# Fused attention and gated feed-forward, one core: second x rows on ScalarE's queue, the rest of the opening in order on SyncE's, short warm-up products up to the transposes, last rows divided at column 384

## Chip, cores, metric

One Trainium2 (trn2) chip, one core. The metric is the device time of the program in microseconds (us). Each chip job also timed the kernel before on its own chip, so comparisons below are made inside one job.

## The reference, cut to what matters

```python
xn = layernorm(x)                       # x: 2048 rows of 640
s  = attention(xn, k_cache, v_cache, wq, wo)   # 32 heads of 192, window 512
g  = silu(B(xn))                        # B: (sigmoid(xn @ w_gate) * (xn @ w_up)) @ w_down
return x + s * g
```

Inputs and output are bfloat16. The kernel starts with the layernorm and the B branch for the first 512 rows, and ends with the projection by `wo`, the product with the gate, and the addition of what is accumulated.

## The kernel before: the parts that the change touches

The opening loads, and the order in which the engines are given work (cut; `...` marks cuts):

```python
def load_x(t, n):
    x = xpool.tile([P, n, D], BF16, ...)
    nc.sync.dma_start(x[:], xf[t * P:(t + n) * P, :]...)
...
nc.vector.memset(warm[:], 0.0)
nc.vector.memset(wg_sb[:, 0, 0:2], 0.0)      # 0.95 to 1.01 us; ScalarE's DMA is issued at 1.06
load_x(0, 1)                                 # SyncE
load_x(1, 1)                                 # SyncE
load_f(nc.scalar, wg_sb, wg_r, 0, 4, 0, 3)   # ScalarE, 384 KB
load_f(nc.sync, wg_sb, wg_r, 0, 4, 3, NCD)
load_f(nc.sync, wu_sb, wu_r, 0, 4, 0, 3)
load_x(2, 1)
load_f(nc.sync, wu_sb, wu_r, 0, 4, 3, NCD)
load_x(3, 1)
...
dummy(18)               # warm-up: 18 products of 256 columns; nothing reads them
stats_half(0, 0); stats_half(0, 1)
stats_end(0)            # aggregate, sqrt on ScalarE, stats_half(1, 0), then the reciprocal
normal(0, ...)          # xn of rows 0
stats_half(1, 1)
turn_pe(0)              # five transposes on TensorE, copies to xnT
dummy(2)
...
m0 = tile_gates(0, 3)   # 20 products with w_gate, 20 with w_up
```

The last four row tiles (`last_rows`) are projected in two halves of 320 columns each. VectorE multiplies each half with the gate (`gated_rows`), and adds the accumulated rows one step later (`stored_rows`), after which the half is written.

The softmax here doesn't subtract the row's maximum and nothing guards it: scores larger than these inputs give would overflow.

## Time and profile before

| | before |
|---|---|
| timed | 924.52 us median of 3 (924.49 to 924.56) |
| the profiled execution | 922.88 us, span 921.08 us |
| PE busy | 913.9 us of 921.1 |
| rows 0 usable / rows 1 used | 3.06 / 4.99 us |
| transposes start / first gate product | 6.01 / 6.92 us |
| last product ends / VectorE ends | 917.14 / 918.48 us |

From the page of the kernel before, the span and the busy time (share of the span, number of instructions):

```profile
span 921.1 us, 25176 instructions
PE 913.9 (99%) x11438; PEld 630.7 (68%) x11456; DVE 490.7 (53%) x983; ACT 302.7 (33%) x333; POOL 132.7 (14%) x157
```

TensorE (PE) is busy nearly throughout; only the two ends can give anything. The timeline of VectorE at the opening of the kernel before (start, duration, engine, line, operation, output<-inputs; in brackets the idle time before it and what ended it):

```profile
3.06 0.89 DVE L198 BATCH_NORM_STATS2 st<-x_sb 128x6 f32<-128x320 bf16 x2 [2.04 <-DMA x_sb<-in_A_x_dram]
3.98 0.21 DVE L203 BATCH_NORM_AGGREGATE mv<-st 128x2 f32<-128x12 f32 x1
4.99 0.49 DVE L198 BATCH_NORM_STATS2 st<-x_sb 128x6 f32<-128x320 bf16 x1 [0.79 <-DMA x_sb<-in_A_x_dram]
5.40 0.15 DVE L208 RECIPROCAL rstd<-rstd 128x1 f32<-128x1 f32 x1
5.58 0.64 DVE L218 TENSOR_SCALAR xn<-x_sb,mv,rstd 128x384 bf16<-128x384 bf16 x2
```

The statistics of rows 1 wait 0.79 us for their DMA, and they stand ahead of the reciprocal that rows 0 need. TensorE over the same time:

```profile
1.06 4.02 PE L190 MATMUL bank<-warm 128*128 128x256 bf16 x18 [1.06 <-DVE eps_t L182]
6.01 0.54 PE L230 MATMUL bank<-ident,xn 128*128 128x128 bf16 x5 [0.93 <-DVE xn L218]
6.92 1.28 PE L300 MATMUL bank<-xnT,wg_sb 128*128 128x128 bf16 x20
8.04 0.83 PE L300 MATMUL bank<-xnT,wu_sb 128*128 128x128 bf16 x12
```

Two things are to be read here. There is a hole of 0.93 us between the warm-up products and the transposes. And the products run at two paces. The 18 warm-up products of 256 columns start 213 ns apart. The 20 gate products of 128 columns take from 6.92 to 8.04, 56 ns apart. The first pace is about half of the second: 256 columns at 56/128 ns each would take about 112 ns. The trace's clock record (kept in the packed trace; no view prints it) has the change between the two: it rises to 1.0 at 5.60 us after the start of the span, and falls to 0.5, 914.772 us after that. "Half clock" below means the slower pace. The changed kernel's trace has the same 914.772 us between rise and fall; three later traces, with a rise at 10 us or after, have 911.359 us there, 3.413 us less. What sets the moment of the rise the traces don't show.

The end of VectorE's work in the kernel before:

```profile
917.20 0.48 DVE L473 TENSOR_TENSOR o_sb<-bank,gate 128x320 f32<-128x320 f32 x1
917.60 0.88 DVE L478 TENSOR_TENSOR gate<-o_sb,acc 128x320 bf16<-128x320 f32 x2
```

After the last product (ended at 917.14) come one product with the gate and two additions of 320 columns.

### The profile page before, as it was taken

To read this page: it belongs to the slowest core of one execution; us is meant where nothing else is said; L and a number is where in the kernel's file an instruction comes from. 1 tells how busy PE (TensorE), PEld (TensorE's weight loads), DVE (VectorE), ACT (ScalarE), POOL (GpSimd) and SP (SyncE) were. 2 spreads that over 40 slices of the span, in tenths; PEclk is the share of its full clock that TensorE was granted. 3 is DMA by queue.
4 is the path that set the end of the run, shared out by engine and by line. 5 is a ranking of instruction groups with operands and counts; after the bars stand their busy time and mean duration, and the time that the engine had idled before them with its cause. 6 is when DMAs were issued, how large, how long until landed. Compare 5 with 4: busy or idle time off the path is not lost.

```text
span 921.1 us, 25176 instructions
## 1 busy us (share of the span) xinstructions
PE 913.9 (99%) x11438; PEld 630.7 (68%) x11456; DVE 490.7 (53%) x983; ACT 302.7 (33%) x333; POOL 132.7 (14%) x157
## 2 busy tenths in 40 slices
PE   8999999999999999999999999999999999999998
PEld 6445455466868686767677777777776767686885
DVE  5452522445646464655555555555464646464667
ACT  4222222254242424233333333242414151515150
POOL 1000100001002000200120011001100111065733
PEclk9999999999999999999999999999999999999999
DMA  9310330115344524352425162526252614263435
GB/s 318 83 28 2 89 86 1 43 62 87 71 70 103 89 55 85 92 100 42 98 79 113 36 104 79 113 30 111 64 106 49 114 61 93 63 116 107 91 80 135
DMA packets 163147, 77.14 MB, mean 84 GB/s; under 512 B 140992, under 2 KB 158608, under 8 KB 163040
## 3 DMA queue, kind: packets, MB, share of 16 engines
q1 hardware_dynamic: 155680, 53.64, 29.8%
q0 software_dynamic: 5808, 20.52, 7.9%
q8 instruction: 89, 1.46, 0.7%
q10 hardware_dynamic: 1552, 1.38, 0.5%
q14 instruction: 18, 0.15, 0.1%
HBM read 39.45 MB, written 2.62 MB: 46 GB/s over the span
## 4 chain that ended last, share of the span: by engine, by line
PE 98%; DVE 1%; DMA 0%; issue 0%; ACT 0%; DVEq 0%; SPq 0%
PE bank L492 22%; PE bank L421 21%; PE bank L443 19%; PE bank L403 18%; PE bank L250 10%; PE bank L262 6%; PE bank L369 1%; PE bank L300 1%; PE bank L526 0%; DMA x_sb<-in_A_x_dram 0%; DVE gate L478 0%; DVE o_sb L473 0%; DVE st L198 0%; PE bank L230 0%; DVE xn L218 0%
## 5 line engine op out<-in xcount | busy, mean ns | idle before, releaser
L407 ACT ACTIVATE E<-bank 128x1024 bf16<-128x1024 f32 x256 | 255.6, 1023 | 456.2 <-PE bank L403 456.1
L421 PE MATMUL bank<-xnT,wq_sb 64*128 64x512 bf16 x1800 | 226.5, 376 | 0.0
L492 PE MATMUL bank<-wo_sb,oT 64*128 64x320 bf16 x2688 | 205.3, 296 | 0.0
L403 PE MATMUL bank<-qT,kT 64*128 64x512 bf16 x1536 | 200.9, 376 | 0.0
L443 PE MATMUL bank<-vbuf,E 64*128 64x193 bf16 x4096 | 195.4, 243 | 0.0
L443 PEld LDWEIGHTS <-E 64*128 64x128 bf16 x4096 | 179.0, 94 | 9.9 <-issue 0.3
L492 PEld LDWEIGHTS <-oT 64*128 64x128 bf16 (+1 forms) x2892 | 164.3, 94 | 29.8 <-issue 0.3
L428 DVE CAST qT<-bank 128x1024 bf16<-128x1024 f32 x90 | 110.2, 1225 | 128.5 <-PE bank L421 128.5
L421 PEld LDWEIGHTS <-wq_sb 64*128 64x128 bf16 x1800 | 106.6, 100 | 86.5 <-issue 0.4
L403 PEld LDWEIGHTS <-kT 64*128 64x128 bf16 x1536 | 88.7, 94 | 72.9
L456 DVE TENSOR_TENSOR o_st<-bank,rden 128x768 bf16<-128x768 f32 x128 | 122.6, 958 | 4.8 <-DMA out_dram<-gate 0.4
L507 DVE TENSOR_TENSOR acc<-bank,acc 128x640 f32<-128x640 f32 x96 | 79.1, 824 | 20.1 <-PE bank L492 20.1
L118 POOL DMA_DIRECT2D vbuf<-in_A_v_cache_dram x28 | 21.1, 755 | 311.0 <-PE bank L443 308.1
L426 DVE COPY seen<-bank 128x2 f32<-128x2 f32 x90 | 14.3, 159 | 79.1 <-PE bank L421 79.1
L455 DVE RECIPROCAL rden<-bank 128x4 f32<-128x4 f32 x128 | 23.4, 183 | 60.4 <-PE bank L443 59.5
L250 PE MATMUL bank<-xnT,wu_sb 128*128 128x512 bf16 x215 | 54.4, 379 | 0.3
L250 PE MATMUL bank<-xnT,wg_sb 128*128 128x512 bf16 x216 | 54.5, 379 | 0.2
L256 DVE TENSOR_TENSOR hT<-bank,sig 128x512 bf16<-128x512 f32 x44 | 30.3, 689 | 42.9 <-ACT sig L253 42.9
L262 PE MATMUL bank<-wd_sb,hT 128*128 128x128 bf16 (+1 forms) x376 | 52.4, 297 | 0.4
L253 ACT ACTIVATE sig<-bank 128x512 bf16<-128x512 f32 x44 | 26.3, 598 | 68.3 <-PE bank L250 66.8
L262 PEld LDWEIGHTS <-hT 128*128 128x128 bf16 x384 | 29.7, 98 | 23.1
L250 PEld LDWEIGHTS <-wu_sb 128*128 128x128 bf16 x220 | 21.5, 98 | 26.0
(56 smaller groups left out, 364.2 us busy)
## 6 DMA issues: line engine op xcount, KB each, us to landing
wo_sb<-in_A_wo_dram SPq DMA_DIRECT2D x7, 960.0 KB, 5.7
wq_sb<-in_A_wq_dram POOLq DMA_DIRECT2D x7, 960.0 KB, 6.2
k_st<-in_A_k_cache_dram POOLq DMA_DIRECT2D x14, 384.0 KB, 5.6
vbuf<-in_A_v_cache_dram POOLq DMA_DIRECT2D x28, 192.0 KB, 3.4
row<-in_A_x_dram POOLq DMA_DIRECT2D x16, 160.0 KB, 3.0
oT<-o_st SPq DMA_TRANSPOSE x128, 3.4
x_sb<-in_A_x_dram SPq DMA_DIRECT2D x3, 640.0 KB, 10.6
wd_sb<-in_B_w_down_dram SPq DMA_DIRECT2D x1, 1920.0 KB, 14.2
```

Source lines behind the costliest of these rows:

```text
L250: nc.tensor.matmul(bank[k][:, half, 0:r1 - r0], lhsT=w[:, c, f * P:(f + 1) * P], rhs=xnT[:, b, c, r0:r1], start=(c == 0), stop=(c == NCD - 1))
L253: nc.scalar.activation(sig[:, 0:r1 - r0], bank[k][:, 0, 0:r1 - r0], AF.Sigmoid)
L256: nc.vector.tensor_tensor(hT[b][:, f, r0:r1], bank[k][:, 1, 0:r1 - r0], sig[:, 0:r1 - r0], ALU.mult)
L262: nc.tensor.matmul(wide(k)[:, d0:d1], lhsT=hT[b][:, f, q * P:(q + 1) * P], rhs=wd_sb[:, f, d0:d1], start=(f == 0), stop=(f == NF - 1))
L403: nc.tensor.matmul(bank[k][:, i, :], lhsT=kT[r, pr, j, c * P:(c + 1) * P], rhs=q[r, pr * DJ + j, :], start=(j == 0), stop=(j == DJ - 1))
L407: nc.scalar.activation(E[u, pr][:, c, :, :], bank[k][:], AF.Exp, scale=scale_qk)
L421: nc.tensor.matmul(bank[k][:, half, :], lhsT=wq[r, c, col:col + DJ * (P - 1) + 1:DJ], rhs=xnT[r, b, c, :], start=(c == 0 and not second), ...
L428: nc.vector.tensor_copy(qT[u][:, 2 * m:2 * m + 2, :], bank[k][:])
L443: nc.tensor.matmul(o4[:, q, 0:DH + 1], lhsT=e[r, c, h % 2, q * P:(q + 1) * P], rhs=vbuf[r, h, c, 0:DH + 1], start=(turn == 0 and qq == 0 a ...
L456: nc.vector.tensor_tensor(o_st[u][:, :, h * DH:(h + 1) * DH], o4[:, :, 0:DH], rden[:].to_broadcast([P, TQ, DH]), ALU.mult)
L492: nc.tensor.matmul(res[:, half, :], lhsT=oT[u][r, cc, q * P:(q + 1) * P], rhs=wo[r, cc, half * HD:(half + 1) * HD], start=(turn == 0 and c ...
L507: nc.vector.tensor_tensor(cols(acc[:, t, :]), res, cols(acc[:, t, :]), ALU.add)
```

## The change

The intent is to have rows 1 earlier, to leave no hole between warm-up and transposes, and to shorten what follows the last product. Rows 1 move to ScalarE's queue and the first gate weights to SyncE's; six short products follow the 18 long ones; the last row tile is cut 384 + 256 instead of 320 + 320, and one more addition goes to GpSimd.

```diff
-        def load_x(t, n):
+        def load_x(t, n, eng=nc.sync):
...
-            nc.sync.dma_start(x[:], xf[t * P:(t + n) * P, :].rearrange("(q p) d -> p q d", p=P))
+            if eng is nc.scalar:
+                nc.vector.memset(x[:, 0, 0:2], 0.0)
+            eng.dma_start(x[:], xf[t * P:(t + n) * P, :].rearrange("(q p) d -> p q d", p=P))
...
-        nc.vector.memset(wg_sb[:, 0, 0:2], 0.0)
         load_x(0, 1)
-        load_x(1, 1)
-        load_f(nc.scalar, wg_sb, wg_r, 0, 4, 0, 3)
+        load_x(1, 1, nc.scalar)
+        load_f(nc.sync, wg_sb, wg_r, 0, 4, 0, 3)
...
         dummy(18)
+        dummy(6, 64)
...
+            cut = HD if q < TQ - 1 else 384
-            for i in range(2):
-                d0, d1 = i * HD, (i + 1) * HD
+            for i, (d0, d1) in enumerate(((0, cut), (cut, D))):
...
-                args = (o, t, d0, d1, nc.vector if q or i else nc.gpsimd, (nc.scalar, nc.sync)[i])
+                wait.append((o, t, d0, d1, nc.gpsimd if n in (0, 4) else nc.vector, (nc.scalar, nc.sync)[i]))
-                while len(wait) > (1 if (q, i) > (0, 0) and (q, i) < (TQ - 1, 1) else 0):
+                while len(wait) > (n in (1, 2, 3, 6)):
```

More of the change, by code (lines that the diff above doesn't have):

```diff
@@ L186, with dummy @@
         nc.gpsimd.memset(vbuf[:, :, :, DH:DH + 2], 1.0)
-        def dummy(n):
+        def dummy(n, cols=256):
             for _ in range(n):
-                nc.tensor.matmul(bank[1][:, 1, 0:256], lhsT=warm[:, 0:P], rhs=warm[:, 0:256],
+                nc.tensor.matmul(bank[1][:, 1, 0:cols], lhsT=warm[:, 0:P], rhs=warm[:, 0:cols],
                                  start=True, stop=True)
@@ L521, in last_rows @@
             o = fin.tile([P, D], F32, name="o_sb", bufs=2)
-            for i in range(2):
-                d0, d1 = i * HD, (i + 1) * HD
-                k = order[(2 * q + i) % 4]
+            cut = HD if q < TQ - 1 else 384
+            for i, (d0, d1) in enumerate(((0, cut), (cut, D))):
+                n = 2 * q + i
+                res = bank[order[n % 4]][:, 0, 0:d1 - d0]
                 for cc in range(GC):
-                    nc.tensor.matmul(bank[k][:, 0, 0:HD],
-                                     lhsT=oT[NU - 1][:, cc, q * P:(q + 1) * P],
+                    nc.tensor.matmul(res, lhsT=oT[NU - 1][:, cc, q * P:(q + 1) * P],
                                      rhs=grp[NG - 1]["wo"][:, cc, d0:d1],
                                      start=(cc == 0), stop=(cc == GC - 1))
-                gated_rows(o, t, d0, d1, bank[k][:, 0, 0:HD])
-                args = (o, t, d0, d1, nc.vector if q or i else nc.gpsimd, (nc.scalar, nc.sync)[i])
-                wait.append(args)
-                while len(wait) > (1 if (q, i) > (0, 0) and (q, i) < (TQ - 1, 1) else 0):
+                gated_rows(o, t, d0, d1, res)
+                wait.append((o, t, d0, d1, nc.gpsimd if n in (0, 4) else nc.vector,
+                             (nc.scalar, nc.sync)[i]))
+                while len(wait) > (n in (1, 2, 3, 6)):
                     stored_rows(*wait.pop(0))
```

## The prediction

> **What bounds it now.** The profile's first part has TensorE (PE) busy 913.9 of 921.1 us; the chain of waits is 98% PE. The timeline shows no PE gap over 0.06 us between 10 us and the end, so only the two ends can give anything, and what PE gains at the opening should reach the end undiminished.
>
> Opening (timeline, chain, waits): x rows 0 are usable at 3.06. The first half statistics of rows 1 wait for their DMA until 4.99 (0.79 us of idle; issue at 1.15, landing 3.8 us later) and stand, in VectorE's order, ahead of the reciprocal (5.40) that rows 0 need. ScalarE's square root was done at 4.53. Then xn 5.58, transposes 6.01 (PE idle 0.93 us after the warm-up products), copy 6.53 to 6.87, first gate product 6.92. The chain shows just this sequence. The packets show why rows 1 are late: ScalarE's queue carries the 384 KB of gate weights issued at 1.06, which share the 16 DMA engines with rows 1 until 4.5; both finish together.
>
> **What changes.** Rows 1 (160 KB) go on ScalarE's queue, the gate weights on SyncE's behind rows 0. [...] At the pace of the ScalarE queue now, 128 packets were through by about 3.5, so I estimate rows 1 landing at 3.9 to 4.3 instead of 4.96. Gate weights still land near 5.3, needed at 6.2.
>
> VectorE then runs statistics of rows 1 right after its aggregate (4.20), reciprocal at about 4.61, i.e. 0.79 earlier; ScalarE's root allows at most 0.84. Transposes could start near 5.22. The warm-up products end at 4.87 (start to start 213 ns, half clock until 5.60 in the profile); six more of 64 columns fill to about 5.2 to 5.5 (estimate, 53 to 107 ns each). If the clock still rises at 5.60, some transposes run at half clock and end at about 5.8 instead of 6.35. So the copy starts near 5.87 and the first gate product near 6.25: 0.65 us earlier. Up-weights (landing 7.12, 8.32) are needed from 7.4 and 8.3, rows 2 and 3 (7.58, 8.77) at 7.6 and 8.8: just in time, a loss of at most 0.1 there, partly absorbed by the 0.13 us wait at 9.73. The DMA stream is full (350 GB/s), so this is where a larger gain would end.
>
> Tail (timeline): last product ends 917.14; then product with the gate (0.40 start to start at 320 columns), two additions (0.40 + 0.48), end 918.48; write landed 920.10; span 921.08. With 384/256 columns these become about 0.34 + 0.47 + 0.42: 0.07 less; moving one addition to GpSimd unloads VectorE where it wasn't late.
>
> **Prediction.** 0.65 + 0.07, about 0.7 us: 923.8 us; range 923.3 to 924.2. Faster by over 2%: 0.005; within 2%: 0.99; slower: 0.005.
>
> **What would show it.** Rows 1's statistics start at 4.2 with no DMA wait; reciprocal 4.6; PE gap before the transposes under 0.3; first gate product 6.2 to 6.3; last product about 0.65 earlier; VectorE's end 1.27 after it (now 1.34).
>
> **What would make it wrong.** Rows 1 land no earlier [...]; the short products run past xn; the clock rises at another time in the timed runs, where continuous products could gain more; up-weights arrive later and PE waits; or the ends vary by some tenths.

## The result

The changed kernel took 922.65 us (median of 4, 922.58 to 922.98), the kernel before 924.54 us (median of 4, 924.49 to 924.91; three of them are those quoted above). The ratio is 0.9979, 95% interval 0.9962 to 0.9997. (A ratio is the mean time of one kernel's fast runs over that of the other's of the same rounds, so not quite the ratio of the medians quoted.) The gain is 1.89 us, where 0.72 had been predicted and 924.2 to 923.3 was the range. Yet the two profiled executions differ by only 0.30 us in the time of the run (922.88 against 922.58), and by 0.27 in the span. The page of the changed kernel:

```profile
span 920.8 us, 25187 instructions
PE 914.8 (99%) x11444; PEld 629.1 (68%) x11462; DVE 491.2 (53%) x982; ACT 302.3 (33%) x333; POOL 133.5 (15%) x158
```

So two questions had to be answered: why the timed runs gained 1.9 us, and why the profiled ones gained 0.3 rather than 0.7. VectorE's timeline of the changed kernel:

```profile
4.05 0.21 DVE L204 BATCH_NORM_AGGREGATE mv<-st 128x2 f32<-128x12 f32 x1
4.17 0.44 DVE L199 BATCH_NORM_STATS2 st<-x_sb 128x6 f32<-128x320 bf16 x1
4.62 0.16 DVE L209 RECIPROCAL rstd<-rstd 128x1 f32<-128x1 f32 x1
```

Rows 1 are there (all 16 parts of the DMA had landed at 3.49, before 4.96) when the aggregate is done; the wait is gone and the reciprocal starts 0.78 us earlier. TensorE's timeline of the changed kernel:

```profile
1.06 4.34 PE L191 MATMUL bank<-warm 128*128 128x256 bf16 x24 [1.06 <-DVE eps_t L183]
5.25 0.71 PE L231 MATMUL bank<-ident,xn 128*128 128x128 bf16 x5
6.20 1.28 PE L301 MATMUL bank<-xnT,wg_sb 128*128 128x128 bf16 x20
7.62 0.84 PE L301 MATMUL bank<-xnT,wu_sb 128*128 128x128 bf16 x12
```

There is no hole before the transposes, and the first gate product starts at 6.20 instead of 6.92. But the up-weight products start at 7.62, only 0.42 earlier than before. The weight loads in the timeline of the changed kernel name the reason:

```profile
7.62 0.67 PEld L301 LDWEIGHTS <-wu_sb 128*128 128x128 bf16 x12 [0.32 <-DMA wu_sb<-in_B_w_up_dram]
8.82 0.45 PEld L301 LDWEIGHTS <-wu_sb 128*128 128x128 bf16 x8 [0.25 <-DMA wu_sb<-in_B_w_up_dram]
```

TensorE now waits twice for up weights, so 0.72 us at the first gate product become 0.40 at the first product of 512 columns (16.98 before, 16.58 after). That lead stays as it is until 200 us. Then 0.15 us are lost near 208 us and 0.11 near 880 us, in waits for which the profile names no releaser ("issue"). With the tail below, 0.40 - 0.26 + 0.08 + 0.04 (the write after VectorE's end) makes 0.26 of the 0.27 us of span.

The end of VectorE's work in the changed kernel:

```profile
916.52 0.93 DVE L475 TENSOR_TENSOR o_sb<-bank,gate 128x384 f32<-128x384 f32 x2
917.37 0.88 DVE L480 TENSOR_TENSOR gate<-o_sb,acc 128x384 bf16<-128x384 f32 x2
```

The last product ended at 916.99, VectorE at 918.25: 1.26 us later, before 1.34.

### The profile page after: what moved, and what is told of

Same layout as the page of the kernel before. It is cut to its first block, busy times and chain, and to the rows that moved or that the text cites. A ratio compares the mean times of both kernels' runs of the same rounds, so it can differ in the third digit from the quotient of the medians.

```text
span 920.8 us, 25187 instructions
## 1 busy us (share of the span) xinstructions
PE 914.8 (99%) x11444; PEld 629.1 (68%) x11462; DVE 491.2 (53%) x982; ACT 302.3 (33%) x333; POOL 133.5 (15%) x158
## 4 chain that ended last, share of the span: by engine, by line
PE 98%; DMA 1%; DVE 0%; SPq 0%; issue 0%; DVEq 0%
PE bank L494 22%; PE bank L423 21%; PE bank L445 19%; PE bank L405 18%; PE bank L251 10%; PE bank L263 6%; PE bank L371 1%; PE bank L301 1%; DMA wu_sb<-in_B_w_up_dram 1%; PE bank L529 0%; DVE o_sb L475 0%; DVE gate L480 0%; SPq L166 0%; SPq L161 0%; PE bank L231 0%
```

## The experiments

The theory formed after the result is the **clock theory**. The hole before the transposes delays the rise of the clock in some executions and not in others. By this theory it did not in the profiled execution of before (the clock rose at 5.60), it did in the timed ones, and there the products after the hole ran at half clock for some time more. The rival is the **data theory**: the gain is that of the order of the loads alone. Every timed kernel below had five runs; before had nine in the same job and on the same chip.

### First job

`b_same`, the kernel before unchanged.

> The kernel before, unchanged. Theory 1 (clock): [...] a profile of a 924.5 us execution shows the clock rising near 9 us, the gate products from 6.9 us at 107 ns start to start instead of 56, and a span of about 922.7; an execution of 922.9 us shows the clock rising near 5.6. Theory 2 (data): the 924.5 us executions have the clock at 5.6 too and lose 1.6 us in waits for the first weights or elsewhere.

Measured: 924.70, 923.49, 924.58, 923.60, 923.13 us; before in the same job 922.87 to 924.74, in two groups: six runs at 922.87 to 923.11, one at 923.83, two at 924.63 and 924.74. The profile fell on the run of 924.70. TensorE's timeline in it:

```profile
1.05 4.02 PE L190 MATMUL bank<-warm 128*128 128x256 bf16 x18 [1.05 <-DVE eps_t L182]
6.57 0.71 PE L230 MATMUL bank<-ident,xn 128*128 128x128 bf16 x5 [1.49 <-DVE xn L218]
7.52 2.33 PE L300 MATMUL bank<-xnT,wg_sb 128*128 128x128 bf16 x20
9.64 1.08 PE L300 MATMUL bank<-xnT,wu_sb 128*128 128x128 bf16 x12
```

The same kernel and the same line: the 20 gate products now take from 7.52 to 9.64, 106 ns apart instead of 56, and the clock record of this trace rises at 10.15. This is what the clock theory asked for (a rise near 9 had been named; it came later). A third of the excess in this execution comes before the slow gate products, though: rows 1 landed at 5.52 instead of 4.96, which widened the hole, and the first gate product was 0.60 later. From the first gate product to the first product of 512 columns it then took 11.31 us instead of 10.06: the clock's part is about 1.25 of 1.85 us. It is the only traced run of the upper group; that the others are like it is inferred from the experiments that follow, and from a number. After that point the two traces run in step to the end.

That number is the mean granted clock, which the record gives for every run to three decimals. It counts half clock only after the first rise: all five runs of `b_hole10` below, whose trace has the rise at 11.75, show 1.000. Of the 32 runs of before that have it (`b_same` included), six show 0.998. All six are in the upper group (14 of the 32); the other eight there show 0.999, and no run outside it is below 0.999. A figure that rounds to 0.998 means about 2.8 us or more at half clock after the first rise (0.0015 of 923 us, doubled), while the end of the kernel accounts for at most 1.61 us in any trace here (`a_third`). So in these six the clock had probably risen early, fell after the hole for 1.2 us or more (2.8 less 1.61), and rose again. The other eight, at 0.999, can have lost at most 2.8 us in this way; a late first rise, as in `b_same` (0.999), fits them. This is an estimate from rounded figures, and no run of the six was traced, but it points to the array's clock in each of the six.

The page's clock row and column (PEclk) don't show a late first rise. In the same trace the view of a stretch of time (in order: us, busy time of PE, PEld, DVE, ACT, POOL, then PEclk, DMA share, GB/s) says:

```profile
1.00:5.00 4.00, 3.94 (x18) 2.55 (x18) 1.11 (x5) 2.20 (x4) 0.37 (x2) 1.00 0.74 220
```

PEclk is 1.00 while the warm-up products start 213 ns apart. The pace of the products, their number against their time, is where it is to be read.

`b_fill`, the hole of before filled, nothing else:

```diff
-        def dummy(n):
+        def dummy(n, cols=256):
...
         dummy(18)
+        dummy(20, 64)
```

> The kernel before with nothing changed but 20 short products (64 columns, about 53 ns each) after the 18 long ones, so that the array is busy from 1.06 us to about 5.95 us, when xn is there. Theory 1 (clock): timed runs fall by about 1.6 us, to 922.7 to 923.0. Theory 2 (data and queue order): no change, 924.5.

Measured: 923.11 to 923.92 (mean 923.53, the same as before's 923.50). No run is at 924 or more (of before, two of nine in this job were, so five runs alone prove little), but the lower group did not appear either, and the stated 922.7 to 923.0 was missed. Its profile (a run of 923.44) has the first gate product at 6.93 and the clock rising at 6.93, the first product of 512 columns at 16.99 as in the profile of before, and then loses 0.31 us near 210 us and 0.27 near 885 us in waits without a named releaser. The experiment is thus half a confirmation, because the waits elsewhere, with instructions added, seemed to cost as much as the filled hole gave. `b_wide` below repeats it without adding any.

`a_nofill`, the changed kernel without its six short products:

```diff
         dummy(18)
-        dummy(6, 64)
```

> The changed kernel without its six short products: the hole before the transposes is about 0.2 to 0.4 us instead of 0. Theory 1: if a hole of this size is already too much [...], 924.2; if only the long hole of before is, as the changed kernel, 922.6 to 922.7. Theory 2 (data): 922.6, the short products do nothing.

Measured: 922.14, 922.27, 922.46, 923.18 and 923.98. Three of five are as the changed kernel, one is 0.2 above its highest run in any job (922.98), and the last is where a late clock rise would put it (`a_hole10` below, with its rise at 11.01, has 923.54 to 924.59). Taken up again below.

`b_tail`, the changed `last_rows` alone:

> The kernel before with the changed last rows alone. All theories: 0.05 to 0.2 us less than before, 924.3 to 924.5; VectorE's end after the last product at about 1.27 us instead of 1.34.

Measured: 922.83, 922.96, 922.96, 924.16, 924.64, two groups as before; the 924.3 to 924.5 expected took all runs for the upper group. The three of the lower group have a median of 922.96, the six of before 923.07. In the profile VectorE ends 1.26 us after the last product (before 1.34), and the span ends 2.55 us after that (before 2.60). The tail is worth 0.1 us and has no part in the groups.

### Second job

`a_again`, the changed kernel unchanged.

> The changed kernel, unchanged, for its spread. Clock theory: no hole in the array's work from 1.06 us on, [...] no run above 923.5, most 922.2 to 923.2, and the ratio to the runs of before depends on how many of those hit the bad phase (924.5 and more). Rival (data order alone): a constant gain on every run of before, bad ones too, so the changed kernel would show two groups as well, about 1.6 us apart.

Measured: 922.02 to 922.52. Before in the same job: 922.97, 923.13, 923.22, and six runs from 924.18 to 925.02. One group against two: the data theory's constant gain is refuted. Its profile had a late clock rise, at 7.01, with this timeline:

```profile
6.21 1.66 PE L301 MATMUL bank<-xnT,wg_sb 128*128 128x128 bf16 x20
7.71 0.83 PE L301 MATMUL bank<-xnT,wu_sb 128*128 128x128 bf16 x12
```

The gate products are slower here (1.66 instead of 1.28 us), but the up-weight products start only 0.09 us later than in the first profile of the changed kernel, because those had to wait for their weights. In this trace a clock that rises as late as 7.01 us is nearly hidden.

`b_hole10`, the kernel before with a larger hole:

```diff
-        dummy(18)
+        dummy(10)
```

> The kernel before with 10 long warm-up products instead of 18, so that the hole before the transposes is about 3.1 us instead of 0.93. Clock theory: [...] the clock rises between about 8.8 and 12.8 us in every run, and every run takes at least 924.3 (up to 926.3); none near 922.9. Rival: the warm-up products do no work that anything waits for, so the times stay as before, most at 923.0.

Measured: 925.14 to 925.92, all five above even the upper group of before; the clock rose at 11.75 in the profile. TensorE's timeline:

```profile
1.06 2.31 PE L190 MATMUL bank<-warm 128*128 128x256 bf16 x10 [1.06 <-DVE eps_t L182]
6.36 0.71 PE L230 MATMUL bank<-ident,xn 128*128 128x128 bf16 x5 [2.99 <-DVE xn L218]
7.31 2.33 PE L300 MATMUL bank<-xnT,wg_sb 128*128 128x128 bf16 x20
9.43 1.48 PE L300 MATMUL bank<-xnT,wu_sb 128*128 128x128 bf16 x12
```

Eight products that compute nothing were taken away, and every run is slower. Nothing reads them; what they are worth is what they do to the clock (rise at 11.75 here, at 5.60 in the profile of before).

`a_hole10`, the changed kernel with the same hole:

```diff
-        dummy(18)
-        dummy(6, 64)
+        dummy(10)
```

> The changed kernel with 10 long warm-up products and no short ones; the early x rows and the tail are kept. Clock theory: clock rises between 8 and 12 us in every run; the cold products hide the 0.55 us of waits for the up weights, so the runs take 923.5 to 925.3, and the profile has no wait for up weights in the first tile. Rival (data order alone): 922.3 to 922.7, like the changed kernel.

Measured: 923.54 to 924.59 (mean 924.08), clock rise at 11.01, and no wait for up weights. It has the early rows 1 and the new tail and still gives back 1.8 us of the changed kernel's mean of 922.25 in this job. It is 1.35 us faster than `b_hole10` (mean 925.43), more than the data order gives elsewhere. In the two profiles its transposes start 1.11 us earlier, and the first product of 512 columns 1.03 us earlier (18.25 against 19.28): at half clock TensorE doesn't wait for the up weights, so little of the lead is given back there.

`a_two_q`, a try at a better version, with the second part of the gate weights on ScalarE's queue too. In the changed kernel's trace the DMAs move 238 GB/s from 3.0 to 3.5 us and 347 from 4 to 5; the try is to fill that dip and have the up weights earlier:

```diff
-        load_f(nc.sync, wg_sb, wg_r, 0, 4, 3, NCD)
+        load_f(nc.scalar, wg_sb, wg_r, 0, 4, 3, NCD)
```

> A try at a better version: the changed kernel with the second part of the first gate weights on ScalarE's queue, behind x rows 1, so that both queues have work from 2.2 us on and the up weights stand one place further forward on SyncE's. [...] the up weights land by 7.3 instead of 7.6, and the time is 0.1 to 0.3 us lower for the same clock rise[...].

Measured: 922.07 to 923.04, no better (the changed kernel in this job 922.02 to 922.52). The dip did go (341 GB/s from 3.0 to 3.5 us, 238 in the changed kernel), and the up weights were late all the same, so the dip was not what held them. The first part of the up weights landed at 7.43 instead of 7.58 or 7.34. It was its last parts that were late, not all of it. This ordinary list gives the times at which the 16 parts of that DMA landed, as the traces record them (cut off, not rounded, at two decimals):

```
before   6.64 6.68 6.76 6.78 6.78 6.79 6.82 6.83 6.87 6.87 6.88 6.89 6.90 6.97 7.08 7.12
changed  6.25 6.43 6.44 6.46 6.49 6.54 6.55 6.56 6.57 6.57 6.58 6.60 6.62 6.66 6.69 7.58
a_again  6.38 6.39 6.40 6.41 6.42 6.45 6.53 6.56 6.61 6.62 6.65 6.67 6.76 6.79 7.14 7.34
a_two_q  6.37 6.41 6.42 6.44 6.49 6.50 6.51 6.52 6.56 6.59 6.68 6.72 6.74 7.17 7.20 7.43
```

Most parts land 0.3 us earlier than before; one to four of 16 lag, and the products wait for the last. In the changed kernel's trace the lag is there one load earlier (the second part of the gate weights: one part at 6.48, the others by 5.55), and every later load up to 13 us has one part about 0.9 us behind the rest, so the second wait for up weights is the same lag. All profiles with the new order of loads show some lag, none with the old order shows one there. In the changed kernel's trace single packets of 0.15 to 0.51 us stand among others of 0.046 us between 4 and 6 us, when the gate weights pass; both traces have such packets from 1.7 to 3.3 us, and before has none between 4 and 6. Why they are slow no run here shows, and it stays open.

### Third job

`a_third`, the changed kernel again, as the measure for the other three.

> The changed kernel again, on the same chip as the three others of this call: by the clock theory 922.0 to 923.1 in every run, no run at 923.5 or above.

Measured: 922.20 to 922.86, mean 922.48; before 922.74 to 924.91, mean 923.74, four of nine at 924.4 or more.

`a_nofill2`, the changed kernel without short products again: can the hole of 0.35 us that is left still bring a run near 924, as one of the first five was (923.98)?

> The changed kernel without its six short products, again. [...] If it can, again one or two of five runs near 924; if not, all below 923.2 and the one at 923.98 had another cause.

Measured: 921.91 to 922.46, mean 922.25. So the remaining hole of 0.35 us (4.87 to 5.22, by the pace of the products; so measured, before has 1.14, and by the profile's modelled ends the two are 0.15 and 0.93) didn't show in these five; in ten runs of both jobs one was at 923.98, of which there is no trace. The six short products are not needed for most of the gain; whether they guard against a rare late rise is not settled. The early rows 1 closed most of the hole by themselves. The short products don't close it always either: in the profile of `a_third` the clock rose at 4.03, the rest of the warm-up ran at full pace and ended sooner, and 0.42 us of hole were left.

`a_wide`, the changed kernel with 18 wider warm-up products in place of 18 + 6:

```diff
-    warm = const.tile([P, 256], BF16, name="warm")
+    warm = const.tile([P, 276], BF16, name="warm")
...
-        dummy(18)
-        dummy(6, 64)
+        dummy(18, 276)
```

> A try at a better version: the changed kernel with the same 18 warm-up products made 276 columns wide (230 ns each at half clock), so that they end at 5.20 us, in place of 18 of 256 and six of 64; the array is as busy, and its instruction count is that of before. If the small waits for nothing visible near 208 and 880 us (0.1 to 0.6 us in all kernels with added warm-up instructions, none in four profiles with the old count) come from the added instructions, they are gone and the runs take 921.9 to 922.4, below the changed kernel by 0.1 to 0.3; if they are chance, the two agree.

Measured: 921.98 to 922.34, mean 922.21, against 922.48 of the changed kernel. The profile has no wait without a releaser near 208 or 880 us. It is 0.27 us below the changed kernel in the mean, but two runs of the changed kernel (922.20 both) lie inside its spread, so five runs each don't settle that it beats it; and it is only 0.04 below `a_nofill2`, which fills nothing, so what the two share, the old number of instructions, is as likely a reason as the filling. As to the waits: seven profiles of kernels whose TensorE has the number of instructions of before (the profile of before, `b_same`, `b_tail`, `b_wide`, `a_nofill`, `a_nofill2`, `a_wide`) have none of 0.06 us or more beyond those of before; of seven with another number, six have 0.09 to 0.87 us. (The record's text, with 0.1 to 0.6 us, leaves out 0.87 in `a_two_q`.) That is a strong association; its cause was not taken apart. One candidate was not tested: in the changed kernel's trace, 16 KB packets of the queue named "instruction" run at 209.8 and 878.8 us, near both waits; but the profile of before has such packets at 210.3 and 878.6 and no wait.

`b_wide`, the kernel before with its hole filled and no instruction added:

```diff
-    warm = const.tile([P, 256], BF16, name="warm")
+    warm = const.tile([P, 332], BF16, name="warm")
...
-        dummy(18)
+        dummy(18, 330)
```

> The kernel before with its 18 warm-up products made 330 columns wide (275 ns each at half clock), so that they fill the array until about 6.0 us with no instruction added: the clock part alone. Clock theory: no run above 923.7 [...], lowest about 922.9, while before on the same chip has runs at 924.2 to 925.0. Rival (data order): same two groups as before.

Measured: 922.82 to 923.46, mean 923.12; before in this job has a mean of 923.74. The upper group is gone and the lower is kept, and this with the data order of before: rows 1 landed at 5.13, no earlier than before. This is the clock's part by itself. With four of nine runs of before in the upper group, five runs would miss it by chance about once in 20; with `b_fill`, ten of ten runs with the hole filled miss it. TensorE's timeline in its profile (clock rise at 5.34; the idle time before the transposes is down from 0.93 to 0.33 us, not to none because rows 1 landed 0.17 us later than in the profile of before, and the gate products are at full pace from the first):

```profile
1.10 4.76 PE L190 MATMUL bank<-warm 128*128 128x330 bf16 x18 [1.10 <-DVE eps_t L182]
6.18 0.54 PE L230 MATMUL bank<-ident,xn 128*128 128x128 bf16 x5 [0.33 <-DVE xn L218]
7.09 1.28 PE L300 MATMUL bank<-xnT,wg_sb 128*128 128x128 bf16 x20 [0.15 <-DVE xnT L234]
```

### All together

| job (one chip each) | before: runs, mean, runs at 924.1 or more | changed: runs, mean, highest | difference of means |
|---|---|---|---|
| result | 4, 924.62, 4 | 4, 922.72, 922.98 | -1.90 |
| second | 9, 924.10, 6 | 5, 922.25, 922.52 | -1.85 |
| third | 9, 923.74, 4 | 5, 922.48, 922.86 | -1.26 |

In the first job, which didn't time the changed kernel, before and `b_same` had four of 14 at 924.1 or more. In all, 18 of 36 runs of the kernel before are in the upper group (mean 924.63), 15 in the lower (mean 923.04) and three between; none of the 14 of the changed kernel is above 922.98. Against the lower group of the same job alone, the changed kernel gains 0.86 us in the second and 0.50 in the third (means 923.11 to 922.25, and 922.98 to 922.48). In the third job the whole 1.26 divides into 0.62 for filling the hole (`b_wide`) and 0.64 for the earlier rows 1 with the tail, of which the tail is about 0.1. The first share is no constant: it hangs on how many of the nine runs of before fell into the upper group.

The traces, one execution each, by the opening that they have (us from the start of the span; the clock rise is from the trace's clock record, "512" is the first product of 512 columns):

| opening | clock rise | first gate product | 512 |
|---|---|---|---|
| before (`b_tail`, profile of before, `b_same`) | 5.08, 5.60, 10.15 | 7.12, 6.92, 7.52 | 17.18, 16.98, 18.83 |
| before, hole filled (`b_wide`, `b_fill`) | 5.34, 6.93 | 7.09, 6.93 | 17.15, 16.99 |
| before, hole of 3 us (`b_hole10`) | 11.75 | 7.31 | 19.28 |
| changed (`a_third`, profile, `a_again`) | 4.03, 5.99, 7.01 | 6.13, 6.20, 6.21 | 16.36, 16.58, 16.65 |
| changed, no short products (`a_nofill`, `a_nofill2`) | 4.25, 5.97 | 6.13, 6.17 | 16.41, 16.38 |
| changed, wide products (`a_wide`) | 6.95 | 6.16 | 16.60 |
| changed, second gate weights on ScalarE's queue (`a_two_q`) | 5.50 | 6.16 | 16.43 |
| changed, hole of 1.9 us (`a_hole10`) | 11.01 | 6.19 | 18.25 |

Within one opening, a rise up to 7 us moves the last column by 0.3 us at most; with a rise at 10 us or later it is 1.6 us or more behind (in `b_same` 0.6 of that from the late rows 1). From the first warm-up product on, the rise came after 3.0 to 6.0 us in eleven traces, and after 9.1 to 10.7 us in three, whose holes are 1.49, 1.87 and 2.99 us (`b_same`, `a_hole10`, `b_hole10`). No rise was seen between 7.01 and 10.15.

## Why the prediction was wrong

The prediction was wrong: 922.65 lies below its range, and the gain was 1.89 instead of 0.72. Point by point:

- **The step that failed** is the sum "0.65 + 0.07, about 0.7 us: 923.8 us", in which a gain read from the profiled execution was taken off the timed 924.52. The profiled execution took 922.88 and was of the lower group; the timed ones were of the upper group and had 1.6 us more to lose. The term for the clock was zero in the sum. The prediction did name it ("the clock rises at another time in the timed runs, where continuous products could gain more") but gave it no weight. What the runs showed in its place: half of all runs of before are about 1.6 us slower; the one of these that was profiled has a clock that rises late (10.15 us against 5.60), and six others have a granted clock of 0.998 on record; `b_wide` removes the upper group with the clock alone, and `b_hole10` puts every run above it.
- **Rows 1** were right, and the size nearly: statistics predicted at 4.2 and started at 4.17, reciprocal 4.61 and 4.62, first gate product near 6.25 and 6.20. They landed even earlier (3.49) than the 3.9 to 4.3 estimated.
- **The short products** were estimated at 53 to 107 ns; they ran 53 ns apart and held up nothing. The transposes, predicted near 5.22, started at 5.25.
- **The up weights**, "just in time, a loss of at most 0.1", were mis-sized: waits of 0.32 and 0.25 us, and 0.72 us of lead became 0.40. One lagging part of 16 set the landing (7.58 instead of the expected 7.12).
- **"What PE gains at the opening should reach the end undiminished"** did not quite hold: 0.26 us went in waits near 208 and 880 us.
- **The tail** was right: 1.26 us after the last product, 1.27 predicted.
- Against the lower group of before, that is with the clock's luck taken out, the changed kernel gained 0.50 to 0.86 us, about the 0.72 predicted for it. That the sum comes so near is partly luck. Its terms, with the up weights and the waits in the middle as measured, give only the 0.27 us by which the two profiles differ, and against the one run of the lower group on the first chip (922.88) the changed kernel's mean gained 0.16.

## What to carry to other kernels

Compare the time of the profiled execution with the timed runs before using a profile as their baseline; a difference of more than their spread means that the profile shows another kind of execution. Warm-up products should reach nearly up to the first real product, since a hole that does no harm in one profile can go with a late clock rise in the next run (before: hole of 0.93 us, rise at 5.60; `b_same`, the same kernel: 1.49 us, 10.15); holes of 0.33 us (`b_wide`) and 0.15 us (`a_nofill2`) showed no harm in five runs each. Widening the products fills a hole without adding instructions. A small load that the first chain waits for should be issued ahead of a large one that is needed later, on a queue where nothing stands before it (here rows 1 landed at 3.49 instead of 4.96, while the DMAs moved 344 GB/s from 2 to 10 us instead of 333), and a lead won there lasts only until the next load that arrives just in time.
